# The last output tile in two pieces, and another order of the jobs, in an attention-plus-MLP kernel on one core

## The chip, the cores and the metric

The kernel runs on one core of one Trainium2 chip. The metric is the device time of one execution in microseconds (us). A result is the median of several executions. The engines are named as in the profile: PE (matmuls; PEld is its weight load), DVE (VectorE), ACT (ScalarE), POOL (GpSimd) and SP (SyncE, which here only issues DMAs).

## The reference

Input x is 2048 tokens by 512 numbers. Two branches read its layer norm `xn`, and the output is x plus both.

```python
# A: 32 heads of 16, four segments of 512 tokens, each with softmax attention inside the segment
# and a linear memory (M, z) of the segments before
logits = einsum("bhqd,bhkd->bhqk", qs, ks) * scale + mask
a_dot = einsum("bhqk,bhkd->bhqd", softmax(logits), vs)
a_mem = (phi(qs) @ M) / (phi(qs) @ z + 1e-6)
o = g * a_mem + (1.0 - g) * a_dot
M, z = M + phi(ks).T @ vs, z + sum(phi(ks))
A = o @ wo
# B: 512 -> 1792 -> 512
B = gelu(layernorm(xn) @ w1 + b1) @ w2 + b2
return x + A + B
```

## The kernel before

**Tiling.** The heads are taken eight at a time, so that there are 16 *units* (unit i is segment i // 4 and head group i % 4), and the MLP is cut into 16 pieces as well (256 tokens by half of the hidden columns). Products that need more than half precision are split in a high and a low f16 part and take three matmuls. A unit passes through these stages: projection of k and q (L583, job `T`), rounding and storing them to DRAM and reading them back as rows (`Tv`, `Tr`), scores for the maximum of each row (L741 on PE, L748 on DVE, job `M`), the row of maxima (L754, `R`, `Rr`), scores again, transposed, with the exponential on ACT (L783, L790, job `S`), the causal mask on POOL (L804, `Sg`), the product with v (L817, jobs `pv` and `PV`), and a chain of six steps over DVE, ACT and POOL that divides, adds the memory term and splits the result (L841 to L854, job `O`). When the four units of a segment are through, `out_jobs` multiplies their results with `wo`: for each of the four tiles of 128 tokens, 12 matmuls of 512 columns into one PSUM tile (L944), one sum on DVE into `acc` (L947), and a store by `save` (L861). The MLP has its own jobs: `D` (L583 on w1), `G` (gelu), `H` (split), `e` (L926), which add to the same `acc` tiles (L930).

**What array form PE uses.** The L741, L783 and L681 matmuls use 48, 50 or 64 of the 128 rows of the array, the L817 and L718 matmuls 32 of the 128 columns. All others use the whole array.

**Head.** In the first 20 us PE has little of its own to do. Two token tiles are normalised by DVE, two by POOL (L534), and PE transposes them (L561, job `Xt`). The weights arrive by DMA in pieces, and PE forms the sums of squares by "traces" of bf16 matmuls (L380, jobs `wm`), from which DVE works out scales (`wf`), before ACT, DVE and POOL split the weights (`ws`). Eight "warm" jobs `W` (L501, four matmuls of the identity each) are put in between.

**What sets the order.** The kernel is scheduled by hand. `streams()` lists chains of jobs; each character of the string `ORDER` takes the next job of one chain, and `plan()` walks through the 1706 characters and emits the instructions of each job on its engines. Within an engine, and in SP's queue of DMAs, that order is the order of execution. Waits between engines are set from the data. The string `BANKS` gives each PSUM tile its bank, one of eight, in the order in which the 948 tiles are taken. [...]

```python
def dense():
    return dps.tile([P, 512], F32, name="dense" + next(banks), bufs=1)
```

## Time and profile before

| | us |
|---|---|
| median of three runs (692.14 to 693.23) | 692.92 |
| the profiled execution, its own time | 692.55 |
| its span, first to last instruction | 690.8 |
| PE busy | 680.1 (98%) |
| DVE busy | 504.6 (73%) |
| ACT busy | 472.2 (68%) |
| POOL busy | 353.1 (51%) |

The profile is of one execution. A line names the kernel's line (L944 is line 944), the engine and the operation, what it writes and reads, with the sizes as partitions by elements, and `x48` says how many instructions it gathers. In a list by time the first number is the start in us, the second the time taken; what stands in square brackets is the idle time of the engine before it and what ended that. "busy" of PE counts a matmul from start to its modelled end. PEclk is the share of the full clock that PE was granted.

### The profile page before, as it was taken

The page shows a single profiled execution, that of the slowest core. Times are in us where ns is not written, and L with a number is a line of the kernel's source. Part 1 is how long each engine was busy: PE and PEld are TensorE (multiplying, and loading weights), DVE is VectorE, ACT ScalarE, POOL GpSimd, SP SyncE. Part 2 cuts the span into 40 slices and gives each one's busy share as a digit, 9 for nine tenths or more (in the row PEclk, how much of TensorE's full clock was granted, in tenths as well). Part 3 has the DMA queues.
Part 4 walks back from the last instruction along what each step waited for, and adds up shares of the span by engine and source line. Part 5 has one row for each costly group of instructions (what it writes and reads, how often), then busy time and mean ns, then how long its engine had stood idle before and what let it go on. Part 6 is the DMA issues. An engine that isn't in the chain of part 4 may idle for free.

```text
span 690.8 us, 15856 instructions
## 1 busy us (share of the span) xinstructions
PE 680.1 (98%) x5855; PEld 393.0 (57%) x5855; DVE 504.6 (73%) x1612; ACT 472.2 (68%) x877; POOL 353.1 (51%) x577
## 2 busy tenths in 40 slices
PE   6999999999999999999999999999999999999997
PEld 5854655657654566755546555565555447465543
DVE  5899978897787669867696786968577475688622
ACT  3688897987766577668836738667865555767970
POOL 7488649575535343564554345434462405438562
PEclk8999999999999999999999999999999999999999
DMA  9888233302321142322221224221402113420101
GB/s 269 264 207 205 97 94 58 99 30 76 76 47 40 34 116 58 107 48 79 69 70 26 77 57 101 70 64 44 105 18 56 55 48 94 102 77 17 18 2 61
DMA packets 52745, 55.84 MB, mean 81 GB/s; under 512 B 4974, under 2 KB 41596, under 8 KB 52668
## 3 DMA queue, kind: packets, MB, share of 16 engines
q1 hardware_dynamic: 50364, 50.64, 26.4%
q0 software_dynamic: 2304, 4.20, 3.8%
q8 instruction: 46, 0.75, 0.5%
q14 instruction: 31, 0.25, 0.1%
HBM read 37.77 MB, written 17.05 MB: 79 GB/s over the span
## 4 chain that ended last, share of the span: by engine, by line
PE 96%; POOL 1%; DVE 1%; issue 0%; POOLq 0%
PE dense L583 40%; PE dense L926 21%; PE dense L817 11%; PE dense L944 6%; PE dense L783 6%; PE dense L741 6%; PE dense L681 2%; PE dense L561 1%; PE dense L380 1%; PE dense L697 1%; PE dense L648 1%; DVE dense L748 1%; PE dense L718 1%; DVE w1s L446 0%; PE dense L754 0%; POOL kst L237 0%
## 5 line engine op out<-in xcount | busy, mean ns | idle before, releaser
L748 DVE CUSTOM_DVE_ANT_0 dense<-dense,mask 128x384 f32<-128x384 f32 (+3 forms) x512 | 233.8, 526 | 39.0 <-PE dense L741 34.4
L790 ACT ACTIVATE pt<-dense,qkcs 128x512 f32<-128x512 f32 (+1 forms) x384 | 204.0, 632 | 35.0 <-PE dense L783 35.0
L926 PE MATMUL dense<-w2s,hT 128*128 128x512 f16 x672 | 166.0, 380 | 0.0
L583 PE MATMUL dense<-xnT,w1s 128*128 128x256 f16 x1344 | 161.2, 273 | 0.0
L804 POOL TENSOR_SCALAR_AFFINE_SELECT pt<-pt 128x256 f32<-128x256 f32 x256 | 102.3, 436 | 108.8 <-ACT pt L790 108.3
L583 PEld LDWEIGHTS <-w1s 128*128 128x128 f16 x1344 | 129.5, 98 | 29.2 <-issue 5.4
L900 POOL TENSOR_TENSOR hT<-hh,hT 128x512 f16<-128x512 f32 x64 | 68.3, 1067 | 95.8 <-ACT hT L898 89.2
L926 PEld LDWEIGHTS <-hT 128*128 128x128 f16 x672 | 61.0, 98 | 67.3 <-issue 13.4
L817 PE MATMUL dense<-pt,vt 128*32 128x512 f32 (+3 forms) x1024 | 77.6, 436 | 0.0
L748 DVE DVE_READ_ACCUMULATOR2_ANT mc<- 128x1 f32 x512 | 72.6, 142 | 0.0
L880 DVE SCALAR_TENSOR_TENSOR hT<-dense,sc,cb 128x512 f32<-128x512 f32 x64 | 43.6, 681 | 34.2 <-PE dense L583 27.7
L898 ACT ACTIVATE hT<-hh 128x512 f16<-128x512 f32 x64 | 37.4, 584 | 27.1 <-POOL hh L896 27.1
L817 PEld LDWEIGHTS dense<-pt,vt 128*32 128x32 f32 x1024 | 30.7, 109 | 41.7 <-issue 31.8
L783 PE MATMUL dense<-qst,kst 50*128 50x384 f16 (+3 forms) x512 | 52.1, 298 | 1.1 <-DVE mc L748 1.1
L896 POOL TENSOR_SCALAR hh<-hT,sc 128x512 f32<-128x512 f32 x64 | 42.1, 658 | 21.2 <-ACT hT L886 17.9
L741 PE MATMUL dense<-kst,qst 48*128 48x384 f16 (+3 forms) x512 | 51.5, 298 | 0.0
L886 ACT ACTIVATE hT<-hT,b1t 128x256 f32<-128x256 f32 x112 | 46.4, 495 | 0.2
L848 POOL TENSOR_TENSOR nN<-nN,oT 128x512 f32<-128x512 f32 x16 | 21.0, 1312 | 49.5 <-DVE oT L660 49.5
L583 PE MATMUL dense<-xnT,wks 128*128 128x512 f16 (+1 forms) x252 | 44.5, 329 | 0.0
L583 PE MATMUL dense<-xnT,wqs 128*128 128x512 f16 (+1 forms) x252 | 44.4, 329 | 0.0
L944 PE MATMUL dense<-wos,oT 128*128 128x512 f16 x192 | 43.8, 379 | 0.0
L583 PE MATMUL dense<-wvs,xnT 128*128 128x512 f16 x192 | 43.8, 379 | 0.0
(230 smaller groups left out, 838.1 us busy)
## 6 DMA issues: line engine op xcount, KB each, us to landing
kst<-kd SPq DMA_DIRECT2D x32, 192.0 KB
qst<-qd SPq DMA_DIRECT2D x32, 192.0 KB
qd<-hl SPq DMA_DIRECT2D x36, 128.0 KB
kd<-hl SPq DMA_DIRECT2D x33, 128.0 KB
acc<-in_A_x_dram SPq DMA_DIRECT2D x16, 256.0 KB
acc<-in_B_b_dram POOLq DMA_DIRECT2D x16, 256.0 KB, 4.2
out_dram<-acc SPq DMA_DIRECT2D x16, 256.0 KB
xt<-in_A_x_dram SPq DMA_DIRECT2D x14, 256.0 KB
```

The source lines that it names most:

```text
L583: T.matmul(p, ws(k, a), xs(k, b), start=i == 0, stop=i == 3 * KT - 1)
L741: T.matmul(p[:, o:o + n], stk[i, 0][r, t, P * qb:P * qb + P], stk[i, 1][r, t, :n], start=True, stop=True)
L748: V.tensor_tensor_reduce(p[:, o:o + n], p[:, o:o + n], mask[:, 512 - n:], 1.0, -3e38, OP.add, OP.max, mc[i][:, 4 * b + t, qb:qb + 1])
L783: T.matmul(p[:, o:o + n], stk[i, 1][r, t, P * kb:P * kb + P], stk[i, 0][r, t, P * kb:], start=True, stop=True)
L790: A.activation(pt[i, 4 * b + t][:, OFF[kb]:OFF[kb] + n], p[:, c:c + n], AF.Exp, scale=qkcs[:, 1, i % NG:i % NG + 1])
L804: G.affine_select(v, v, pattern=[[0, 2], [1, P]], compare_op=OP.is_ge, fill=0.0, base=0, channel_multiplier=-1)
L817: T.matmul(p[32 * c:32 * c + 32, P * kb:], vt[s, kb][:, 4 * g + c, 16 * odd:16 * odd + 32], pt[i, 2 * c + odd][:, OFF[kb]:OFF[kb] + LEN[kb ...
L880: V.scalar_tensor_tensor(hzs[fh][:, f0:f + 1, :], p[:, :256 * n].rearrange("p (f c) -> p f c", f=n), col(CG + fh), cbt[hf].unsqueeze(1).to ...
L886: A.activation(hzs[j % 2][:, f, :], hzs[j % 2][:, f, :], AF.Gelu_apprx_tanh, bias=b1t[:, fo:fo + 1])
L900: G.tensor_tensor(hT[:, z, 1, :], hht[j, c], hT[:, z, 0, :], op=OP.subtract)
L926: T.matmul(p, t[:, u, P * a:P * a + P], w2s[:, fo, v, :], start=fi == 0 and n == 0, stop=fi == FH - 1 and n == 2)
L944: T.matmul(p, o[:, u, P * b:P * b + P], wos[:, g, v, :], start=i == 0, stop=i == 3 * NG - 1)
```

## The change

The last of the 16 token tiles is summed and stored in two pieces, 384 and 128 columns: for each piece 12 matmuls of that width into its columns of one PSUM tile, one DVE sum and one store. The other 15 tiles stay as they were. The strings `ORDER` and `BANKS` are replaced; they hold the same jobs, 961 of which have work for PE, in another order.

```diff
 ORDER = (
-    "oamakrkkhbckkkk0h0bihehceddhff220ff22qhjkk2n1h1662gkkrp6237s7lg3k783w8th88999!x9u#k!w7#9$4$vRRv9R$9!3#R!#%k4J5"
...
-    "UICCYAVAABYATYYBYAQUYYBCVCTUCCDEVYFYYGHYYIYYYYYYMMMZMZZZ"
+    "hoaak0khkhhh0rbbrckkd2e01ffc22id2nkh2effgkk261km6jpk6l273k7sg37uhhw8878J899!k#9tw9$9$xW!v#R9vRR$R!#4%x9!3%#RR&"
...
+    "UCCCYVAAYAYTAYBAYYBBQYCCCUCVYTYDUVYEYYYYFGHYIYYYMMZZMMZZ"
 )
...
+    def halves(tok):
+        return (slice(0, 384), slice(384, 512)) if tok == 4 * NSEG - 1 else (slice(0, 512),)
+
     def save(tok):
-        Q.dma_start(out[P * tok:P * tok + P, :], acc[tok])
+        for c in halves(tok):
+            Q.dma_start(out[P * tok:P * tok + P, c], acc[tok][:, c])
...
                 tok = 4 * s + b
                 p = dense()
-                i = 0
-                for g in range(NG):
-                    o = oT[NG * s + g]
-                    for u, v in ((0, 0), (0, 1), (1, 0)):
-                        T.matmul(p, o[:, u, P * b:P * b + P], wos[:, g, v, :], start=i == 0, stop=i == 3 * NG - 1)
-                        i += 1
                 t = acc[tok]
-                V.scalar_tensor_tensor(t, p, col(CO), t, op0=OP.mult, op1=OP.add)
+                for c in halves(tok):
+                    i = 0
+                    for g in range(NG):
+                        o = oT[NG * s + g]
+                        for u, v in ((0, 0), (0, 1), (1, 0)):
+                            T.matmul(p[:, c], o[:, u, P * b:P * b + P], wos[:, g, v, c], start=i == 0, stop=i == 3 * NG - 1)
+                            i += 1
+                    V.scalar_tensor_tensor(t[:, c], p[:, c], col(CO), t[:, c], op0=OP.mult, op1=OP.add)
```

PE's jobs at the start, in the old order: five `W`, two `Xt`, traces of the second k and q pieces, the first scale, two `Xt`, two traces, `W`, the transposes of L524, a trace, `W`, the two traces of wv, a trace, the first projection. In the new order: five `W`, the trace of the second k piece, the first scale, two `Xt`, three traces, `W`, a trace, two `Xt`, the first projection, a trace, the two traces of wv, the transposes of L524. At the end, PE's order is the same from the last `pv` on.

On the other queues the new order moves, among others: on POOL both fills of `kst` (L237) ahead of the statistics of x; on SP the six loads of the second half of `w1` (L315, L308) from ahead of unit 0's row loads (L643) to behind unit 1's q stores (L622 to L624).

## The prediction

> **What bounds the kernel now.** I read the page first, then the waits of PE, then the chain that ended last.

> ```profile
> span 690.8 us, 15856 instructions
> PE 680.1 (98%) x5855; PEld 393.0 (57%) x5855; DVE 504.6 (73%) x1612; ACT 472.2 (68%) x877; POOL 353.1 (51%) x577
> ```

> PE is busy for 680.1 of 690.8 us; no other engine passes 73%. The 10.7 us without PE are in the waits and in the tail:

> ```profile
> PE dense L561 <- DVE xt L532: 2.8, 1, 2.8
> PE dense L501 <- POOL ident masks.py:199: 1.4, 1, 1.4
> PE dense L783 <- DVE mc L748: 1.1, 1, 1.1
> PE dense L561 <- POOL nN L534: 0.9, 1, 0.9
> PE dense L380 <- DMA wqs<-in_A_wq_dram: 0.3, 1, 0.3
> ```

> Four of the five (5.4 us) lie before 13 us; past that, one wait of 1.1 us is left. The last 36 us of the chain (start, us, what):

> ```profile
> 661.07 0.75 PE dense L926 x3
> 661.83 0.33 PE dense L783 x4
> ...
> 676.05 2.37 PE dense L944 x11
> ...
> 678.47 8.17 PE dense L944 x37
> 686.64 0.02 issue
> 686.67 0.75 DVE acc L947
> ```

> PE runs without a gap to 686.64, and 4.2 us follow (690.8 - 686.64). A new order therefore has little to win in the middle. It can move the head, the 1.1 us wait and the tail, and it can change what PE itself spends.

> **Part 1: the number of switches of PE's array.** From the rows above: an L944 matmul of 512 columns takes 2.37/11 = 0.215 us, and L926 has the same form, so three are 0.65; 0.75 passed before L783 (50 rows of the array) began, 0.10 more. The four L783 matmuls run two abreast, two pairs of 256 columns, so about 2 x 0.108 = 0.22; 0.33 passed before L926 went on, 0.11 more. Going to a part of the array and coming back each cost 0.10. I sorted the jobs in the two order strings by what they use: all of the array; 48, 50 or 64 rows (L741, L783, L681); 32 columns (L817, L718). The old order changes class 281 times in 961 PE jobs, the new one 289 times: whole to rows 105 to 109, rows to whole 110 to 114, whole to or from columns 23 to 27, rows to or from columns 43 to 39. Eight more at 0.10 is **+0.8 us**, all on the path, since PE has no slack there. Bounds 0.7 to 0.9.

> **Part 2: the tail.** Rows of VectorE (count, shortest/median/longest ns), of the chain and of the tail's windows (PEclk, DMA share and GB/s end the row):

> ```profile
> L947 DVE SCALAR_TENSOR_TENSOR acc<-dense,sc,acc x16: 746/751/752, 216.0 to 686.7; 128x512 f32<-128x512 f32 x16
> ```

> ```profile
> L382 DVE SCALAR_TENSOR_TENSOR dense<-dense,ident x5: 293/300/333, 16.7 to 33.0; 128x128 f32<-128x128 f32 x5
> ```

> ```profile
> 18.51 1.31 PE dense L583 x12
> ...
> 29.66 1.60 PE dense L380 x28
> ```

> ```profile
> 688.20:689.20 1.00, 0.00 (x0) 0.00 (x0) 0.00 (x0) 0.00 (x0) 0.00 (x0) 0.95 0.70 262
> ```

> The last tile's 12 matmuls of 512 columns (2.59 us) become 12 of 384, 0.162 each by their columns, and 12 of 128, 0.057 each by the L380 row (1.60/28): 1.95 + 0.68 = 2.63, so +0.04. The final VectorE sum falls from 0.75 to 0.30; the 384 columns take 0.60 between these rows. The final store falls from 256 to 64 KB. All 256 KB passed in the last window, at 0.70 share, so a quarter saves about 0.6 us.

> *If PE writes the second piece while VectorE reads the first:* last matmul 686.68, sum done 687.0 against 687.42, transfer 0.6 shorter, less some 0.2 behind the first piece's 192 KB: -0.8. *If the second piece waits for that read,* since both lie in one 512-column tile: first piece ends at 686.0, its read at 686.63, then 0.05 handover, 0.68 of matmuls and 0.16 for the last to run out; sum done at 687.86, 0.44 later than now, less 0.6: -0.2. If the small transfer were no shorter: +0.4. No row shows an engine reading a tile that PE still writes: all 16 L947 begin after their tile's last matmul. That is nearest to the waiting case: **-0.2**, bounds -0.8 and +0.4.

> [...]

> **Part 3: the head.** PE's rows, and the windows (PE busy and PEclk matter):

> ```profile
> 1.43 4.45 PE L501 MATMUL dense<-ident 128*128 128x256 bf16 x20 [1.43 <-POOL ident masks.py:199]
> 8.63 1.09 PE L561 MATMUL dense<-ident,xt 128*128 128x128 f32 x8 [2.76 <-DVE xt L532]
> 10.28 0.61 PE L380 MATMUL dense<-wqs 128*128 128x128 bf16 x4 [0.32 <-DMA wqs<-in_A_wq_dram]
> 12.14 1.12 PE L561 MATMUL dense<-ident,nN 128*128 128x128 f32 x4 [0.93 <-POOL nN L534]
> 13.04 1.06 PE L561 MATMUL dense<-ident,nD 128*128 128x128 f32 x4
> 13.90 1.06 PE L380 MATMUL dense<-pt 128*128 128x128 bf16 x8
> 14.76 1.06 PE L501 MATMUL dense<-ident 128*128 128x256 bf16 x4
> 15.61 0.64 PE L524 MATMUL dense<-ident,stats 128*128 128x128 f32 x2
> ...
> 17.01 0.62 PE L380 MATMUL dense<-wvs 128*128 128x128 bf16 x8
> ```

> ```profile
> 3.00:6.40 3.40, 2.88 (x14) 1.71 (x12) 2.06 (x5) 0.00 (x0) 3.02 (x6) 1.00 0.98 283
> 6.40:9.80 3.40, 1.17 (x12) 1.14 (x12) 2.11 (x6) 1.92 (x5) 2.94 (x9) 1.00 1.16 304
> 9.80:13.30 3.50, 2.25 (x15) 2.01 (x13) 3.27 (x9) 0.62 (x3) 3.25 (x9) 0.51 1.23 295
> 13.30:16.70 3.40, 3.40 (x24) 3.03 (x23) 1.49 (x4) 1.61 (x4) 1.74 (x2) 0.50 1.06 349
> 16.70:20.10 3.40, 3.38 (x41) 3.05 (x40) 3.29 (x19) 1.18 (x2) 0.00 (x0) 1.00 1.17 286
> ```

> ```profile
> 8.45 0.63 ACT L351 ACTIVATE wqs<-wqs 128x512 bf16<-128x512 f32 x1 [0.15 <-DMA wqs<-in_A_wq_dram]
> ```

> The new order puts the trace of wk's second piece and the first scale ahead of the first x transposes. ACT took wq's first piece off the DMA at 8.45 and PE wq's second at 10.28; the piece between lands about halfway, 9.37. So PE idles from 5.88 to 9.37, 3.5 us in place of 2.76, but then finds work: four more traces and a warm-up now run ahead of the second x pair. From starts of rows at half clock: a trace 0.43, a warm-up and a group of four transposes 0.86 each. The new list to the end of the fourth group is 0.3 (trace, half of it at full clock) + 0.4 (scale) + 4 x 0.86 + 4 x 0.43 + 0.86 = 6.7, ending at 16.1. PE comes to the second pair at 14.4; POOL, which now fills both kst buffers before it, delivered it at 12.14 and has 2.2 us to spare. The old order had that work, and the L524 pair of 0.43 besides, done at 15.61 + 0.43 + 0.43 = 16.5: even within 0.1, *at the same clock*.

> The clock decides. Windows with 2.88 and 3.40 us of PE work were followed by the full clock, those with 1.17 and 2.25 by half. New, the window from 9.8 is full of work, nearest to the row with 3.40, so full speed would come at 13.3, not 16.7: 1.7 us of work won, but wv's late landing clips it. Its traces (L380 on wvs, and the one on pt behind it) ran from 17.01 to 18.1 and can hardly end earlier; by then the new order has the first projection (1.31) and one more trace (0.23) done, and owes the L524 pair and a warm-up (0.77): 0.7 to 0.8. I take **-0.7**; bounds -1.7 and +1.7 (half clock for a window more).

> ```profile
> 9.80:13.30 3.50, 1.16 (x6) 1.17 (x7) 0.51 1.23 295
> 13.30:16.70 3.40, 0.81 (x4) 0.41 (x2) 0.50 1.06 349
> ```

> These are the same windows for L561 alone (PE busy first). If its transposes do not count, the old windows held 2.25 - 1.16 = 1.1 (half stayed) and 3.40 - 0.81 = 2.6 (opened); the new ones, with two groups each, 3.4 - 1.7 = 1.7, between the two.

> [...] The rows fit both readings.

> **Part 4: waits in the middle, and moves on the queues.**

> ```profile
> 68.01 2.50 DVE L446 SCALAR_TENSOR_TENSOR w1s<-w1s,sc 128x512 f16<-128x512 f32 x1
> ```

> ```profile
> 30.74 1.89 SPq L315 DMA_DIRECT2D w1s<-in_B_w_dram  x2
> 39.42 0.56 SPq L624 DMA_DIRECT2D qd<-ame  x1
> ```

> ```profile
> 49.41 1.49 ACT L351 ACTIVATE w1s<-w1s 128x1536 bf16<-128x1536 f32 x1
> ```

> The 1.1 us wait on mc came behind this L446, 2.50 us long where an L947 of as many columns takes 0.75; on VectorE it stands ahead of unit 1's fourth maximum, and so it does in the new order. I leave it at 0, bounds -1.1 and +1.1 (one more like it). On SP the six loads of w1's second half move behind unit 0's row loads and unit 1's q stores, from 30.74 to about 40. At 270 GB/s the 1.8 MB (four of 320 KB, two of 256) land by 48; ACT's first use, behind which the v copies queue, is at 49.4 now. Covered, with 1 to 2 us left.

> **Sum.** +0.8 - 0.2 - 0.7 + 0 = -0.1. The profiled execution took 692.55 us, 1.75 more than its span, and 0.37 less than the median of the three runs, 692.92. Against the median: **692.8 us, no change**. I count 0.2% (1.39 us) as what a measurement can tell.

> **Rivals.**
> 1. *Faster:* the tail overlaps (-0.8), the L446 is quick (-1.1), the clock opens early (-0.7): with +0.8, -1.8, 691.1. For: 2.50 is far above 0.75. Against: three things at once.
> 2. *Slower, the clock stays down:* a second window at half from 16.7 to 20.1, head +1.7: 0.8 - 0.2 + 1.7 = +2.3, 695.2. It decides if 1.7 us of work without transposes is too little. For: 2.25 with transposes did not open it. Against: 3.40 with them did.
> 3. *Slower, a new wait:* a maximum or a v copy late on VectorE or ACT holds up PE, as in the wait on mc, twice more: 2 x 1.1 - 0.1 = +2.1, 695.0. For: some covers shrank; unit 15's fifth score job has four PE jobs behind it before its result is read, six before. Against: the old order had one such wait in 670 us.
> 4. *The split shortens nothing* (tail +0.4): +0.5, 693.4, within the forecast's reach.

> **Chances.** Forecast, with rival 4: 0.50 (own range 691.6 to 694.2); rival 1: 0.17; rival 2: 0.18; rival 3: 0.15. Faster 0.17, same 0.50, slower 0.33. The range reaches to rival 1 and to rivals 2 and 3: 691.0 to 695.2.

> **What would show it.** PE busy up by 0.8 less what the clock gives; the second piece's L944 group starting only after the first L947 of the last tile; PEclk 1.00 from 13.3 us (right), 0.50 to 16.7 or 20.1 (wrong); no wait on mc or on w1s over 1.1 us. The forecast is wrong if PE's waits past 20 us sum to over 2 us, or the clock is not full by 17 us.

## The result and the profile after

| | before | after |
|---|---|---|
| median, run side by side | 692.5 (22 runs, 691.27 to 693.54) | 693.34 (22 runs, 692.26 to 694.81) |
| ratio | | 1.0015, 95% interval 1.0009 to 1.0021 |
| profiled execution | 692.55 | 692.92 |
| its span | 690.8 | 691.2 |

The change costs 0.8 us by the medians, 0.6 to 1.5 us by the interval. That is under the 0.2% (1.39 us) that the forecast counted as no change, but not nothing. The forecast was 692.8 us, 0.1 us under the three runs known then, so 0.9 us are to be explained.

From the page of the kernel after, the span and the busy times; then the waits of PE from 0.2 us on (total, times, longest):

```profile
span 691.2 us, 15889 instructions
PE 680.6 (98%) x5867; PEld 394.7 (57%) x5867; DVE 503.5 (73%) x1613; ACT 473.0 (68%) x877; POOL 351.7 (51%) x577
```

```profile
PE dense L380 <- DMA wks<-in_A_wk_dram: 3.7, 1, 3.7
PE dense L501 <- POOL ident masks.py:199: 1.4, 1, 1.4
PE dense L783 <- DVE mc L748: 0.9, 1, 0.9
PE dense L950 <- DVE acc L952: 0.7, 1, 0.7
PE dense L412 <- DVE gr L978: 0.2, 1, 0.2
```

PE is busy 0.5 us longer, and the listed waits sum to 6.9 us where the five of before summed to 6.5. (Behind line 860 the numbers are now 4 to 6 higher: L926 is L930, L944 is L950, L947 is L952, L861 is L865.) The new wait on L952 is the last tile's second piece; the wait on wk stands where that on x stood.

To see where the time goes I took PE's start times at three places at which the TensorE jobs already done are the same in both orders, but for one group of four transposes (L648, 0.44 us from its start to the next) that the new order has behind it at the first place. (A name like e.1.0.1 or T.1.0 is a job's letter with the numbers of the piece that it works on.) PE's rows by time, of before and of after:

```profile
26.91 0.81 PE L583 MATMUL dense<-xnT,wqs 128*128 128x512 f16 x3
111.00 1.47 PE L926 MATMUL dense<-w2s,hT 128*128 128x512 f16 x6
668.70 7.35 PE L926 MATMUL dense<-w2s,hT 128*128 128x512 f16 x33
```

```profile
26.41 1.46 PE L583 MATMUL dense<-xnT,wqs 128*128 128x512 f16 x6
110.56 2.12 PE L930 MATMUL dense<-w2s,hT 128*128 128x512 f16 x9
666.77 2.36 PE L817 MATMUL dense<-pt,vt 128*32 128x512 f32 x32
669.06 7.30 PE L930 MATMUL dense<-w2s,hT 128*128 128x512 f16 x33
```

| us | before | after | difference |
|---|---|---|---|
| start to unit 1's q projection (after: 26.41 - 0.44) | 26.91 | 25.97 | -0.94 |
| from there to e.1.0.1 | 84.09 | 84.59 | +0.50 |
| from there to behind the last unit's values | 557.70 | 558.50 | +0.80 |
| from there to the end of the span | 22.1 | 22.1 | 0.0 |

(The row at 666.77, the last unit's second values, is needed further down.) In this pair of executions the start wins 0.94 us, and the rest gives back 1.3. The tail, which the forecast had at -0.2, is level. Its rows in the kernel after:

```profile
686.43 0.62 DVE L952 SCALAR_TENSOR_TENSOR acc<-dense,sc,acc 128x384 f32<-128x384 f32 x1 [1.20 <-PE dense L950]
687.10 0.83 PE L950 MATMUL dense<-wos,oT 128*128 128x128 f16 x12 [0.71 <-DVE acc L952]
687.97 0.35 DVE L952 SCALAR_TENSOR_TENSOR acc<-dense,sc,acc 128x128 f32<-128x128 f32 x1 [0.92 <-PE dense L950]
```

The second piece's matmuls start 0.05 us after the first sum's end (686.43 + 0.62), not behind the first piece's matmuls. The last sum ends at 688.32, 0.90 later than the 687.42 of before, of which 0.36 was carried in; the span ends 2.9 us behind it instead of 3.4.

### The profile page after: what moved, and what is told of

The parts are those of the page before. It is cut to its first block, busy times and chain, and to the rows that moved or that the text cites. A ratio compares the mean times of both kernels' runs of the same rounds, so it can differ in the third digit from the quotient of the medians.

```text
span 691.2 us, 15889 instructions
## 1 busy us (share of the span) xinstructions
PE 680.6 (98%) x5867; PEld 394.7 (57%) x5867; DVE 503.5 (73%) x1613; ACT 473.0 (68%) x877; POOL 351.7 (51%) x577
## 4 chain that ended last, share of the span: by engine, by line
PE 93%; DVE 2%; DMA 2%; issue 1%; SPq 0%; ACT 0%; POOL 0%; POOLq 0%; DVEq 0%
PE dense L583 39%; PE dense L930 20%; PE dense L817 11%; PE dense L783 6%; PE dense L741 6%; PE dense L950 6%; PE dense L681 2%; PE dense L561 1%; DMA wks<-in_A_wk_dram 1%; PE dense L697 1%; DMA qst<-qd 1%; PE dense L648 1%; DVE dense L748 1%; PE dense L380 1%; PE dense L718 1%
## 5 line engine op out<-in xcount | busy, mean ns | idle before, releaser
L748 DVE CUSTOM_DVE_ANT_0 dense<-dense,mask 128x384 f32<-128x384 f32 (+3 forms) x512 | 233.9, 527 | 35.5 <-PE dense L741 33.4
L930 PE MATMUL dense<-w2s,hT 128*128 128x512 f16 x672 | 168.8, 380 | 0.0
L583 PE MATMUL dense<-xnT,w1s 128*128 128x256 f16 x1344 | 160.7, 273 | 0.0
L804 POOL TENSOR_SCALAR_AFFINE_SELECT pt<-pt 128x256 f32<-128x256 f32 x256 | 100.2, 415 | 116.9 <-ACT pt L790 116.7
L583 PEld LDWEIGHTS <-w1s 128*128 128x128 f16 x1344 | 129.3, 98 | 30.5 <-issue 5.7
L904 POOL TENSOR_TENSOR hT<-hh,hT 128x512 f16<-128x512 f32 x64 | 66.9, 1046 | 103.0 <-ACT hT L902 91.2
L930 PEld LDWEIGHTS <-hT 128*128 128x128 f16 x672 | 60.6, 98 | 64.7 <-issue 13.5
L817 PE MATMUL dense<-pt,vt 128*32 128x512 f32 (+3 forms) x1024 | 76.6, 435 | 0.1
L748 DVE DVE_READ_ACCUMULATOR2_ANT mc<- 128x1 f32 x512 | 73.7, 144 | 0.0
L817 PEld LDWEIGHTS dense<-pt,vt 128*32 128x32 f32 x1024 | 31.8, 109 | 40.9 <-issue 29.8
L900 POOL TENSOR_SCALAR hh<-hT,sc 128x512 f32<-128x512 f32 x64 | 43.9, 686 | 21.3 <-ACT hT L890 13.4
L783 PE MATMUL dense<-qst,kst 50*128 50x384 f16 (+3 forms) x512 | 52.1, 298 | 0.9 <-DVE mc L748 0.9
L741 PE MATMUL dense<-kst,qst 48*128 48x384 f16 (+3 forms) x512 | 52.2, 298 | 0.1
L950 PE MATMUL dense<-wos,oT 128*128 128x512 f16 (+2 forms) x204 | 43.9, 367 | 0.8 <-DVE acc L952 0.7
L583 PE MATMUL dense<-xnT,wks 128*128 128x512 f16 (+1 forms) x252 | 44.5, 329 | 0.0
L583 PE MATMUL dense<-xnT,wqs 128*128 128x512 f16 (+1 forms) x252 | 44.4, 328 | 0.0
L583 PE MATMUL dense<-wvs,xnT 128*128 128x512 f16 x192 | 44.0, 379 | 0.0
```

Source lines behind the costliest of these rows:

```text
L583: T.matmul(p, ws(k, a), xs(k, b), start=i == 0, stop=i == 3 * KT - 1)
L741: T.matmul(p[:, o:o + n], stk[i, 0][r, t, P * qb:P * qb + P], stk[i, 1][r, t, :n], start=True, stop=True)
L748: V.tensor_tensor_reduce(p[:, o:o + n], p[:, o:o + n], mask[:, 512 - n:], 1.0, -3e38, OP.add, OP.max, mc[i][:, 4 * b + t, qb:qb + 1])
L783: T.matmul(p[:, o:o + n], stk[i, 1][r, t, P * kb:P * kb + P], stk[i, 0][r, t, P * kb:], start=True, stop=True)
L804: G.affine_select(v, v, pattern=[[0, 2], [1, P]], compare_op=OP.is_ge, fill=0.0, base=0, channel_multiplier=-1)
L817: T.matmul(p[32 * c:32 * c + 32, P * kb:], vt[s, kb][:, 4 * g + c, 16 * odd:16 * odd + 32], pt[i, 2 * c + odd][:, OFF[kb]:OFF[kb] + LEN[kb ...
```

## The experiments

The kernels ran in four groups of four, each beside runs of the kernel before on the same chip: 692.5, 692.53, 692.59 and 692.59 us. Orders that are put together from two are cut at an entry of the plan; what one order has not done at the cut follows in the other's order, and the banks go with the jobs. The place where the two meet is called the seam.

### The split or the order

```diff
 new_one: the new ORDER and BANKS
-        return (slice(0, 384), slice(384, 512)) if tok == 4 * NSEG - 1 else (slice(0, 512),)
+        return (slice(0, 512),)
 old_split: the change's halves(), save() and out_jobs(), the old ORDER and BANKS
```

> The new order with the last tile in one piece. Theory A (the order costs, the split is neutral: head -0.4 over many executions, 8 more switches +0.8, more short waits past 27 us +0.4): +0.8 us against before, the same as the whole change. Theory B (the wait of the last tile's second piece costs, its sum ends 0.5 us later by itself, and the order costs nothing): within 0.3 us of before.

> The old order with the last tile in two pieces. Theory A: the second piece waits about 0.7 us for the first sum, its own sum ends some 0.5 us later, the last store is some 0.5 us shorter: 0.0 us against before, within 0.2. Theory B: +0.5 to +0.9 us.

Measured: the new order alone 693.42 us, ratio 1.0015 (1.0006 to 1.0024); the split alone 692.63 us, 1.0005 (0.9997 to 1.0014). The order carries the loss, and the split does nothing that can be told from the times. The waits of the split alone hold the same row as the change:

```profile
PE dense L950 <- DVE acc L952: 0.7, 1, 0.7
```

### Cut at unit 1's q projection: a test that failed

```diff
 newhead_oldrest
+ORDER: the new one to T.1.0 (about 27 us), then the old one; one piece
 oldhead_newrest
+ORDER: the old one to T.1.0, then the new one; one piece
```

> The new order up to unit 1's q projection (26 us), the old order for all that is left, one piece. Theory A: the head gains 0.4 us over many executions, up to 0.9 in those whose clock opens early, so -0.4 us against before. Rival C (the new head is worth nothing, since PE idles 3.7 us in place of 2.8 and the clock is a matter of luck in both): 0.0, within 0.2.

> The old order up to unit 1's q projection, the new order for the rest, one piece. Theory A: +1.2 us (0.8 of switches, 0.4 of short waits). Rival C: +0.8, the whole difference of the change.

Measured: 694.99 us, ratio 1.0037 (1.0027 to 1.0048), and 697.25 us, 1.0072 (1.006 to 1.0085). Both are slower than either whole, which no theory of the parts allows; the waits show the seam. Of the first and of the second kernel:

```profile
PE dense L583 <- DVE ame L621: 2.2, 1, 2.2
```

```profile
PE dense L648 <- DVE phk L635: 3.0, 1, 3.0
PE dense L583 <- DVE ame L621: 1.4, 1, 1.4
```

At 27 us the two orders are far apart on VectorE, and PE waits for the jobs left over there. These two say nothing of the question.

### Cut at 59 us

```diff
 new_to52_old
+ORDER: the new one's first 174 entries, then the old one; one piece
 old_to52_new
+ORDER: the old one's first 174 entries, then the new one; one piece
```

At 174 entries both orders have done the same TensorE jobs. (By the traces this is 59 us into the span; the 52 of the names and of the expectations is the sum of PE's work to there.)

> The first 174 entries of the new order (to H.0.3.2, about 52 us into the span, where the two orders have done the same jobs but one constant fill), then all that is left in the old order; one-piece last tile. Theory A (the start gains a little, the rest loses by switches of the array's form and short waits): the start alone is worth about -0.3, so 692.2 us (691.8 to 692.6), no wait at the seam over 0.5 us. Rival B (the start is where the loss is, because it waits longer for wk's second piece): 693.3 us (693.0 to 693.8).

> The mirror image: the first 174 entries of the old order, then all that is left in the new order; one-piece last tile. Theory A: 8 more switches (+0.8) and new short waits (+0.4) without the start's gain, so 693.7 us (693.3 to 694.2). Rival B: 692.5 us (692.1 to 692.9), since the rest is then neutral.

Measured: 692.97 us, ratio 1.0008 (0.9999 to 1.0018), and 692.14 us, 0.9993 (0.9984 to 1.0001). That is nearer to B in both, though the traces had put the loss past 59 us. The waits of the two, first of new_to52_old, then of old_to52_new, show why: the wait on mc at 70 us, 1.1 in the kernel before, moved as well.

```profile
PE dense L783 <- DVE mc L748: 1.7, 1, 1.7
PE dense L741 <- DMA qst<-qd: 0.3, 1, 0.3
```

```profile
PE dense L741 <- DMA qst<-qd: 0.4, 1, 0.4
PE dense L783 <- DVE mc L748: 0.2, 1, 0.2
```

From 59 to 111 us PE takes 51.34 us in the old order, 51.36 in the new, 51.97 in the first of these two and 50.31 in the second. So the new middle behind the old start wins 1.0, which hides what its rest loses; the first one loses 0.6 in the same place.

### What a change of class costs

The forecast's +0.8 was 0.10 us for each of 8 more changes of the array's form. Here 54 are added by moving 27 jobs past one neighbour:

```diff
 old_moresw, one of 27
-e.2.1.4
 S.2.6
+e.2.1.4
```

> The old order with 27 pairs of neighbours exchanged, one of the score or maximum jobs of 64-row matmuls against one of the feed-forward jobs of full-array matmuls, so that the class of matmul changes 335 times instead of 281; the matmuls are the same. Theory A (0.10 us for each change of class, from the groups of both traces): +5.4 us, 697.9 us (697.0 to 699.0). Rival (the time between two classes is part of waits that go elsewhere when the changes move): within 0.7 us of the kernel before, 691.9 to 693.2 us.

Measured: 698.57 us, ratio 1.0083 (1.007 to 1.0096), 6.0 us more. PE's rows of this kernel at the two places above:

```profile
110.32 1.47 PE L926 MATMUL dense<-w2s,hT 128*128 128x512 f16 x6
660.50 2.12 PE L926 MATMUL dense<-w2s,hT 128*128 128x512 f16 x9 [0.55 <-DVE rc L690]
674.05 2.33 PE L926 MATMUL dense<-w2s,hT 128*128 128x512 f16 x10
```

From 110.32 to 674.05 are 563.73 us, 6.03 more than the 557.70 of before; less the 0.55 of a new wait, that is 5.5 / 54 = **0.10 us** for each. The term of the forecast is right in size and shown to be a cause. (By the rows, L754 uses 32 columns and L969 14 rows, so not all other matmuls use the whole array, as was said above. With these two counted the changes are 313 and 321, still 8 more.)

### A bank of its own for the second piece

```diff
 old_ownbank: old_split with one more bank (that of Qt.15, long idle)
-                p = dense()
                 t = acc[tok]
                 for c in halves(tok):
+                    p = dense()
                     i = 0
```

> The old order with the last tile in two pieces, but the second piece sums into a PSUM bank of its own instead of the other 128 columns of the first piece's bank. Theory A (the second piece waited 0.7 us because the first sum still read that bank): no wait ahead of the second piece, its 12 matmuls run beside the first sum, and the kernel gains about 0.7 us: 691.8 us (691.4 to 692.2). Rival (the wait is for the tile or for VectorE itself, or the two collide elsewhere): a wait of about 0.7 us stays and the time is 692.6 us (692.3 to 693.0).

Measured: 691.95 us, ratio 0.999 (0.9982 to 0.9999). The row of the wait on L952 is gone, and the two sums stand in one row:

```profile
685.39 1.02 DVE L952 SCALAR_TENSOR_TENSOR acc<-dense,sc,acc 128x384 f32<-128x384 f32 x2 [1.20 <-PE dense L950]
```

The second sum now follows at once on the first. From behind the last unit's values to the end are 21.83 us, 0.3 less than before, and the same in the three other kernels that have it (21.77 to 21.79); the times say 0.6. The second piece writes other columns than VectorE reads, and needs no data of it, so the wait of the change is for what the two pieces share: one PSUM tile, and with it one bank. No run has two tiles in one bank, so which of the two sets the wait is not shown.

### Cut at 111 us, and the gains put together

```diff
 new_to111_old
+ORDER: the new one's first 332 entries, then the old one; one piece
 old_to111_new
+ORDER: the old one's first 332 entries, then the new one; one piece
 new52to111
+ORDER: the old one's first 174 entries, the new one's to 332, then the old one; one piece
 new52to111_own
+as new52to111, last tile in two pieces with two banks
```

> The first 332 entries of the new order (to about 111 us, where both orders have done the same TensorE jobs), then all that is left in the old order, its PSUM banks renamed so that they fit; one-piece last tile; 281 changes of class. Theory A (the traces: the stretch from 111 us to the last unit's values is 0.9 us longer in the new order, 0.8 of it the 8 changes of class, and what comes ahead of 111 us is about even): 692.6 us (692.2 to 693.0). Rival B (the times of the two halves cut at 52 us: the loss comes ahead of 52 us): 693.3 us (693.0 to 693.8).

> The mirror image: the first 332 entries of the old order, then the new order; one-piece last tile; 289 changes of class. Theory A: 693.4 us (693.0 to 693.8), and in the trace 557.5 us from the start of e.1.0.2 to that of PV.15.1 instead of 556.5. Rival B: 692.4 us (692.0 to 692.8).

> The old order but for the stretch from 52 to 111 us, which stands in the new order; one-piece last tile; 281 changes of class. Theory A: the run with the old order to 52 us and the new one behind it took 692.14; without the new order's 0.9 us past 111 us this one takes 691.3 us (690.9 to 691.8), with a wait on mc of 0.2 to 0.5 us instead of 1.4 in the trace. Rival B (the new order is neutral past 111 us): 692.1 us (691.8 to 692.5).

> The same order with the last tile in two pieces, the second in a PSUM bank of its own. If the two gains add up: 0.6 us under the run before it, 690.7 us (690.2 to 691.3) by theory A, 691.5 us (691.1 to 691.9) by rival B.

| | median, us | ratio | 59 to 111 us | 111 us to the last values |
|---|---|---|---|---|
| new_to111_old | 693.24 | 1.0012 (1.0002 to 1.0022) | 51.32 | 558.38 |
| old_to111_new | 693.58 | 1.0015 (1.0005 to 1.0025) | 51.48 | 558.97 |
| new52to111 | 692.62 | 1.0005 (0.9996 to 1.0014) | 50.31 | 558.00 |
| new52to111_own | 691.80 | 0.999 (0.9981 to 0.9998) | 50.31 | 558.58 |

The last two columns are start to start of PE's rows, as above. A's number fits the second kernel, B's the first and the last, and the third lies above both. The last column again shows a seam, not the orders: the old order past 111 us takes 557.5 to 557.7 us where it stands whole, and 0.3 to 1.1 more in the three kernels that enter it at 111 us. A row of the last kernel, just behind the cut:

```profile
112.39 0.40 PE L741 MATMUL dense<-kst,qst 48*128 48x256 f16 x4 [0.41 <-ACT pt L790]
```

This maximum takes a bank that the scores just ahead of it, in the other order, had filled. With 0.8 us for the seam taken off, new_to111_old stands at 692.4, where A had it, and old_to111_new without its 0.5 at 693.1. That is an argument from the traces, not a measured time.

### Changes of class taken back, and an earlier row read

```diff
 new_fewsw: the new order with the old one's last 82 entries, and
-Q.4
 T.5.0
+Q.4
...
-e.12.0.4
 Q.14
+e.12.0.4
 new_qearly: the new order with
+Tv.0.0
 ws.1a.3.0
...
-Tv.0.0
-A.0.0
...
 Tr.0.0
+A.0.0
```

> The new order with its changes of class brought back from 289 to 281: the last 82 entries in the old order (4 fewer), and two of the memory-read jobs of 64-row matmuls (Q.4, Q.14) put beside others of their class (4 fewer), banks renamed behind each; one-piece last tile. Theory A (the changes of class make the stretch past 111 us long): 0.8 us under the new order in one piece, 692.6 us (692.2 to 693.1), and 555.8 to 556.9 us from e.1.0.2 to PV.15.1 instead of 557.5. Rival (short waits come in their place): 693.4 us (693.1 to 693.9).

> The new order with the first unit's low query half on VectorE put ahead of the third split of w1 (one entry, about 1.8 us earlier), and the load of the first residual tile on SP's queue put behind the row reads of the first unit. Theory A (the row reads of qst, issued at 35.1 us instead of 33.8, are what the first maxima wait for): issued by 33.6 us, no wait of L741 on qst (0.3 to 0.6 us in the new order), 693.0 us (692.6 to 693.3). Rival (the scores at 70 us wait for VectorE's maxima in any case): the wait on qst goes, the wait on mc of 1.0 us grows by as much, 693.4 us (693.1 to 693.9).

new_fewsw took 701.59 us, ratio 1.0127 (1.0113 to 1.0142): neither theory. Two rows by time, VectorE's and PE's, and PE's windows:

```profile
186.12 0.68 DVE L621 SCALAR_TENSOR_TENSOR hl<-dense,hl 128x512 f16<-128x512 f32 x1
186.95 4.50 PE L817 MATMUL dense<-pt,vt 128*32 128x512 f32 x32 [6.43 <-DVE hl L621]
```

```profile
186.00:190.00 4.00, 3.05 (x20) 1.01 (x24) 0.80 (x3) 0.00 (x0) 0.00 (x0) 0.50 0.12 33
```

With Q.4 moved behind T.5.0, and the banks renamed there, the values of unit 3 took the bank in which T.5.0's result still stood. VectorE read it (L621) only at 186.12, behind six maxima, and PE stood still for 6.43 us. Then the clock was down to half (PEclk 0.50 in the window), and the 32 matmuls took 4.50 us where such 32 took 2.36 in the row at 666.77 above. The run doesn't say what 8 changes of class fewer are worth; it says what a bank's next user can cost.

new_qearly took 692.95 us, ratio 1.0009 (1.0001 to 1.0018), 0.5 under the new order in one piece, where A had it; the intervals of the two ratios overlap, so the times alone don't prove this gain. SP's queue and PE, first of the new order in one piece, then of new_qearly:

```profile
32.90 0.45 SPq L908 DMA_DIRECT2D acc<-in_A_x_dram  x1
...
35.38 0.79 SPq L643 DMA_DIRECT2D qst<-qd  x2
...
41.02 0.82 PE L741 MATMUL dense<-kst,qst 48*128 48x512 f16 x7 [0.41 <-DMA qst<-qd]
```

```profile
35.23 0.79 SPq L643 DMA_DIRECT2D qst<-qd  x2
36.06 0.44 SPq L904 DMA_DIRECT2D acc<-in_A_x_dram  x1
...
40.28 0.82 PE L741 MATMUL dense<-kst,qst 48*128 48x512 f16 x8
```

The read of qst is not issued at 33.6, as I had expected, but at 35.23: SP's queue stood at it for 1.7 us until the store of q had landed (0.9 us in the new order). The wait is gone all the same. What changed is the load of the residual tile, 256 KB, which now stands behind the read and not ahead of it. In the kernel before it also stands behind, and the read is issued earlier:

```profile
33.79 0.86 SPq L643 DMA_DIRECT2D qst<-qd  x2
...
35.76 1.18 SPq L904 DMA_DIRECT2D acc<-in_A_x_dram  x1
```

How much of the half microsecond is the load's and how much the earlier low half's, this run does not separate. In nine of the sixteen traces without the first cut, new_qearly's among them, the first eight maxima take 0.76 us from their start to the next job. The other seven are the five that begin with the new order and have the load ahead of the read (0.99 to 1.55 us), and old_to52_new and old_to111_new (1.51 and 1.55), where the load stands behind it. So the load ahead is not the only thing that makes the read late.

### A kernel that beats both

```diff
 best0: new52to111_own
-behind 111 us M.2.4 takes a bank that the scores ahead of it have just filled
+behind 111 us the banks are renamed, so that M.2.4 takes one that is free for longer
 best: best0 with three swaps like
-e.4.1.0
 Q.6
+e.4.1.0
```

> The order of new52to111_own (old to 52 us, new to 111 us, old behind it; last tile in two pieces with two banks), with the banks behind the seam at 111 us renamed otherwise, so that M.2.4 takes none that the scores before it have just filled. Theory A (the seam's waits of 0.5 to 1.0 us are those of the banks): 691.1 us (690.6 to 691.6), a stretch from 111 to 379 us of 267.9 to 268.1 us instead of 269.0. Rival (the seam's wait is of the order of the jobs and stays): 691.8 us (691.5 to 692.2).

> The same with three memory-read jobs (Q.6, Q.8, Q.11) put beside other jobs of 64-row matmuls: 275 changes of class instead of 281. Theory A (0.10 us each): 0.6 us under best0, 690.5 us (690.0 to 691.1). Rival (Q.6, Q.8 and Q.11 then wait for their banks): the time of best0 or 0.2 us more.

best0: 691.66 us, ratio 0.9986 (0.9977 to 0.9995), 0.9 under the kernel before and 1.7 under the changed one; from 111 us it still took 558.10 us, 0.5 less than new52to111_own, so the renamed banks took part of the seam's wait away, and the time is nearer to the rival's 691.8 than to A's 691.1. best: 692.19 us, 0.9995 (0.9986 to 1.0004): six changes of class fewer, 0.6 by their price, and two new waits among its rows:

```profile
PE dense L681 <- ACT nD L826: 0.7, 1, 0.7
PE dense L681 <- ACT pt L790: 0.4, 1, 0.4
```

They cost 1.1. The three jobs that were moved beside others of their class now come before their banks are free, as the rival had it.

## Why the forecast was wrong

**What bounds the kernel** stood: PE is at 98%, and every loss found is either its own time or a wait of PE.

**Part 1, changes of class, +0.8:** right. All 8 more lie past 111 us (258 there instead of 250), where the new order takes 558.5 us (four traces: 558.47 to 558.51) and the old one 557.5 to 557.7 (three traces); the price was confirmed by adding 54.

**Part 2, the tail, -0.2:** the mechanism was right (the second piece waits 0.71 us for the first sum, the final sum comes late, the store is shorter), the size a little off: 0.0. The last sum ended 0.54 us later (0.90 less the 0.36 carried in) instead of 0.44; the small sum took 0.35 instead of 0.30, and the first one ended 0.06 later than forecast. The store won 0.5 instead of 0.6 in this trace, but not in that of old_split, where the span ends 3.3 us behind the last sum, and the tail is 22.55 us. The 0.71 us of the row, and its absence with a bank of its own (old_ownbank), bear out the waiting case, which the forecast had taken as the nearest to the sums' rows; whether the shared bank or the shared tile sets the wait, they leave open.

**Part 3, the head, -0.7, is the step that failed.** The +0.6 to +1.5 us of the result, less the 0.8 to 1.0 that lie past 111 us and a level tail, leave -0.4 to +0.7 for all that stands ahead of 111 us, where the forecast had -0.7. The chain of it was right: PE waits longer at first (3.73 us against 2.76, for wk), then has more work, and the clock opens earlier. But the forecast took the windows of one execution, 13.3 and 16.7 us, for fixed. They lie elsewhere in each. From sixteen traces, all but those of the first cut, with the time from which the clock stayed full and the start of unit 1's q projection (the new start less 0.44; us):

```
old start  full from  12.5   13.9   16.0   16.4   16.7   17.0   17.0   17.3   18.0   18.0
           T.1.0 at   25.93  26.14  26.44  26.68  26.91  26.95  26.83  27.03  27.38  27.44
new start  full from  13.8   14.1   14.3   14.4   14.8   16.3
           T.1.0 at   25.97  26.16  26.20  26.24  26.67  27.31
```

The means are 16.3 and 14.6 us for the clock and 26.77 and 26.43 us for the projection. So by these means the new start gains **0.3 us, not 0.7**. The times within a row differ by 0.5 us (standard deviation), so the 0.3 is uncertain by some 0.5 either way, and these traces alone don't exclude 0.7; the two traces of the first cut, 26.09 with the new start and 26.77 with the old, would not change it. The gain seems to come through the clock: in the two pairs with the same opening, 13.8 and 13.9, 16.3 and 16.4, the new start is 0.2 ahead and 0.6 behind. The profiled pair, at 16.7 and 13.8, had shown 0.94, more than the forecast; that is the luck of one pair.

**Part 4, waits at no cost, failed in a smaller term.** The wait on mc stayed near 1 us, as forecast. What I hadn't costed is the residual tile's load, which the new order puts ahead of the row reads of unit 0 on SP's queue. The first maxima then wait for qst, and take 0.2 to 0.8 us longer; in new_qearly, with the load behind the read and the low half earlier, they don't. Two traces with the old start wait as well, so the load is a likely cause and not the only one. From 27 to 59 us the six traces with the new start take 33.0 to 33.5 us, 33.2 on average; of the ten with the old start six take 32.8 and four 33.0 to 34.5, 33.1 on average.

The terms now: head -0.3, first maxima +0.1 by these averages to +0.5 by the profiled pair, changes of class with 0.1 of short waits +0.9, tail 0.0; +0.7 to +1.1, against +0.84 by the medians. Of the rivals, none came: three gains at once did not (1), the clock did not stay at half until 20.1 us (2), no second wait of 1.1 us appeared (3), and the split cost nothing that the times show, rather than 0.4 (4). That the +0.5 of rival 4 lies nearest to the result is chance. The signs that were to show the forecast wrong did not show it either: the clock was full from 13.8 us, and the listed waits past 20 us sum to 1.6 us, under the 2 that were named (2.1 with the 0.5 that the first maxima took longer). The loss is made of terms below 1 us that the forecast had cancelling each other; the one of +0.8 came, and the gains against it mostly did not.

**What stays open.** L446 on VectorE, ahead of unit 1's fourth maximum, takes a different time in each order, and the wait on mc follows it. Its rows in the kernels before, after and best0, the first and the last with rows of POOL beside them:

```profile
68.01 2.50 DVE L446 SCALAR_TENSOR_TENSOR w1s<-w1s,sc 128x512 f16<-128x512 f32 x1
67.86 0.97 POOL L448 TENSOR_SCALAR w1s<-w1s,sc 128x512 f32<-128x512 f32 x1
68.52 1.43 POOL L452 TENSOR_TENSOR wks<-pt,wks 128x512 f16<-128x512 f32 x1
69.99 1.16 POOL L804 TENSOR_SCALAR_AFFINE_SELECT pt<-pt 128x256 f32<-128x256 f32 x2
```

```profile
67.90 2.29 DVE L446 SCALAR_TENSOR_TENSOR w1s<-w1s,sc 128x512 f16<-128x512 f32 x1
```

```profile
68.19 1.59 DVE L446 SCALAR_TENSOR_TENSOR w1s<-w1s,sc 128x512 f16<-128x512 f32 x1
67.81 1.42 POOL L452 TENSOR_TENSOR w1s<-w1s 128x512 f16<-128x512 f32 x1
```

The waits of PE behind it were 1.05, 0.87 and 0.17 us. What stretches it was not tried, but the traces point at POOL. Of the 414 executions of L446 in the 18 traces, the 104 with nothing on POOL beside them took 0.74 to 0.75 us, and each one above 0.8 us had POOL at work for at least 0.3 us of its time; some with POOL beside them were as quick as those without. No run moves POOL's work alone. Nor does a run show what 8 fewer changes of class would win without new waits.

## What to carry to other kernels

When an order is searched anew, count what it makes the bounding engine pay per switch of form (0.10 us here), and check each load that moves ahead of a read on its queue; a start that looks better in one trace is to be judged over several, since the clock's windows fell differently from trace to trace (full from 12.5 to 18.0 us in the sixteen above). Before a buffer is cut in two for overlap, give the second part a bank of its own (here worth 0.3 us by the trace, 0.6 by the times). An order put together from two is only as good as its seam: look there first for waits, and don't read the parts' worth from the sum.

## What the runs showed of the hardware

```profile
9.12:12.53 3.41, 3.15 (x20) 3.00 (x19) 1.88 (x7) 1.55 (x4) 3.22 (x8) 0.50 1.22 290
12.53:15.94 3.41, 3.07 (x38) 2.70 (x36) 3.09 (x15) 2.51 (x5) 2.39 (x4) 1.00 1.05 349
```

```profile
9.12:12.53 3.41, 1.97 (x10) 1.57 (x9) 0.50 1.22 290
```

```profile
3.30:6.71 3.41, 2.58 (x13) 1.51 (x10) 2.49 (x6) 0.00 (x0) 2.96 (x5) 1.00 0.95 276
```

```profile
8.58 1.97 PE L561 MATMUL dense<-ident,xt 128*128 128x128 f32 x8 [2.71 <-DVE xt L532]
```

```profile
11.22:14.63 3.41, 3.04 (x20) 2.90 (x18) 2.74 (x9) 1.09 (x3) 3.30 (x8) 0.50 1.13 341
14.63:18.04 3.41, 3.41 (x25) 2.92 (x23) 1.98 (x9) 1.75 (x4) 0.50 (x1) 0.50 1.13 308
```

The first window held 3.15 us of work, 1.97 of it transposes, and the full clock followed. The window of new52to111 held 2.58 us without any transpose, and it did not: the eight transposes behind it took 1.97 us, against the 1.09 in the kernel before, whose window then was at full clock for most of them. (The 1.00 in that row is what is printed ahead of the first record of the clock.) Had only the other 1.18 us counted, the first window could not have opened it. The last two rows, of old_to52_new, speak against counting in full: 3.04 us of work, again with 1.97 of transposes, left the clock at half, though in the kernel before a window with 2.88 us and no transposes was followed by full clock. How much of a transpose's time counts, the runs don't show.

**A wait can cost twice.** In new_fewsw PE's stop of 6.43 us in the middle of the run was followed by half clock (PEclk 0.50) and by 2.1 us more for the next 32 matmuls (4.50 us against 2.36).
